# Step 14 of the attention alone with its own banks, first weight pieces two steps later, exponents on ScalarE beside the MLP

## The chip, the cores and the metric

The kernel runs on one core of one Trainium2 chip. The metric is the device time of one execution in microseconds (us); three runs of the kernel before gave a median of 999.9 us.

## The reference

Linear attention with random features over 4 batches, 8 heads, 576 positions and 64 dimensions, then two MLPs over the 2304 tokens of 512 values:

```python
def phi(x):
    proj = np.einsum('bhsd,md->bhsm', x, omega)          # m = 128
    h = proj - np.sum(x * x, axis=-1, keepdims=True) / 2.0
    return np.exp(h - np.max(h, axis=-1, keepdims=True)) / np.sqrt(m)
q_p, k_p = phi(q * scale), phi(k * scale)
kv, z = np.einsum('bhsm,bhsd->bhmd', k_p, v), np.sum(k_p, axis=2)
x = np.einsum('bhsm,bhmd->bhsd', q_p, kv) / (np.einsum('bhsm,bhm->bhs', q_p, z)[..., None] + 1e-06)
x = x.transpose(0, 2, 1, 3).reshape(2304, 512)
h = x @ w_in                                             # 512 x 2048
x = (np.maximum(h, 0.0) + alpha * np.minimum(h, 0.0)) @ w_out
out = ((x @ w_a) * (x @ w_b)) @ moe2_w_out               # 512 x 1536, back to 512
```

The weights reach the kernel as 64-bit floats, and every MLP product is made of three 32-bit matmuls: high by high, high by low and low by high part.

## The kernel before

The order of the program is the order of each engine: nothing is reordered behind the text. So what stands ahead in the code stands ahead in each engine's queue.

**Weights.** The 68 weight pieces (128x512 doubles, 512 KB) are fetched by SyncE into `raw` (three buffers) and decoded to a pair wh, wl by `Decoder.piece`. A double is two 32-bit words, L and H. `start` makes z from H by a multiplication with 2^-112 on GpSimd (POOL, L126). `piece` then goes on: VectorE (DVE) shifts z (L144), puts the sign in (a, L148), takes the exponent alone (c, L150) and scales L by it (c, L152); ScalarE (ACT) rounds a to wh (L154); POOL, or VectorE where the planner says so, makes a - wh (L155) and wl (L156). `D_.go(3)` takes up to three of a piece's four parts, `D_.go()` one more; `D_.step(x)` gives a step the credit of x pieces. z of the next piece is started as soon as the shift of the one before is issued.

**Attention.** It runs in steps of one tile of 128 positions for k and one for q (a q tile runs 6 steps or more behind the k tile). A step is: `attn_1`, projections into a pair of PSUM banks (pp, L543); `a_max`, the maxima of each part on VectorE (nm, L552); `loads`, the fetches that belong to the step; `a_exp`, exponentials on ScalarE (ph, L566); `attn_2`, parts of a weight piece, kv matmuls (L579), the quotient num/den (nd L613; rc, rc, xn on VectorE L617 to L620), the transposes of q's features (tp L594) and their copy phT (L597 on VectorE or L599 on ScalarE); `attn_3`, the transposes of the result (xp L632) and their copy into xT (L638 on VectorE, L640 on ScalarE).

**Banks.** Five shared banks (`psp`) hold pp, tp, nd, xp and later the MLP's h in turn. In the stage of the attention alone there are two more (`psx`), which the even steps take for their pp; when that stage ends they become the MLP's y.

**Stages.** Steps below `SPLIT_AT` = 14 run alone. Then the first MLP goes over chunks of 256 tokens (`A.run`), and `inside` puts one attention step into each of its f-steps: maxima and exponentials stand between the leaky step h (L285) and the parts gh, gl (L296, L293). Before that, the chunk of x is split into xh (ScalarE, L245) and xl (VectorE or POOL, L248). Behind 140 us mostly, a second program part runs the rest of the MLPs over chunks of 512 ("X phase").

**The planner.** `pick` chooses among engines by a running sum of estimated work: the way whose most loaded engine is least loaded. `passed` lets time go by. A change of an estimate so changes later choices.

Of the kernel before, what the change touches and what calls it, by code (L numbers as in the profile page):

```python
# [9 lines left out]
F32 = mybir.dt.float32  # L10
F32R = mybir.dt.float32r
U32 = mybir.dt.uint32
AF = mybir.ActivationFunctionType
ALU = mybir.AluOpType
# [4 lines left out]
P = 128  # L19
# [9 lines left out]
TT = 5  # L29
VC = 4 * (D + 1)  # L30
EPS = 1e-6
SPLIT_AT = 14
WARM = 7
Q_LAG = 6
CI = 256
# [6 lines left out]
NS = 28  # L42
NS1 = 20

DEC0 = (0.0, 0.3, 0.5)
DEC1 = 1.0
RATE_A = 0.55
RATE_A2 = 0.5
# [5 lines left out]
def tile_kernel(ctx: ExitStack, tc: tile.TileContext, qT, kT, v1, omT, wbits, alpha, out):  # L54
# [44 lines left out]
    class Decoder:  # L99


        def __init__(self):
            self.free = {}
            self.raw = {}
            self.ready = 0
            self.next = 0
            self.credit = 0.0
            self.gen = None
            self.z = {}
            self.ahead = True  # L110

        def load(self, p, after=False):
            if p < NP and p not in self.raw:
# [6 lines left out]
        def start(self, p):  # L120

            if p >= NP or p in self.z:
                return
            self.load(p)
            z = dec.tile([P, DM], U32, tag="z", name=f"z{p}")
            nc.gpsimd.tensor_scalar(out=z.bitcast(F32), in0=self.raw[p][:, :, 1].bitcast(F32), scalar1=2.0 ** -112,  # L126
                                    scalar2=None, op0=ALU.mult)
            load["pool"] += 0.8
            self.z[p] = z

        def piece(self, p):
# [86 lines left out]
    class Mlp:  # L218
# [20 lines left out]
        def split(self, ph, o, n, k):  # L239
            if (ph, o, k) in self.xs:  # L240
                return
            src = xT[:, k, o:o + n]
            hi = self.px.tile([P, self.cap], F32R, tag="xh", name=f"xh{ph}_{o}_{k}")[:, :n]
            lo = self.px.tile([P, self.cap], F32R, tag="xl", name=f"xl{ph}_{o}_{k}")[:, :n]
            nc.scalar.activation(hi, src, AF.Copy)  # L245
            load["act"] += n / 1000
            way = pick({"dve": 1.2 * n / 1000}, {"pool": 2.5 * n / 1000})
            (nc.vector, nc.gpsimd)[way].tensor_tensor(out=lo, in0=src, in1=hi.bitcast(F32), op=ALU.subtract)  # L248
            self.xs[ph, o, k] = (hi, lo)

# [416 lines left out]
    def loads(s):  # L667
        if s < 4:

            if s == 0:  # L670
                load_k(1)
            elif s == 1:
                D_.load(0, True)
                load_q(0)
            elif s == 2:
                load_v(1)
            elif s == 3:
                D_.load(1, True)
                load_q(1)
        elif s in ev["k"]:  # L680
            u, t = ev["k"][s]
            if t == 0 and u + 1 < U:
                load_k(u + 1)
            if t == 2 and u + 1 < U:
                load_v(u + 1)
        if s in ev["q"]:
            u, t = ev["q"][s]
            if t == 4 and u + 2 < U:
                load_q(u + 2)
# [32 lines left out]
    if True:  # L722
# [3 lines left out]
        for s in range(SPLIT_AT):  # L726
# [2 lines left out]
            pj = attn_1(s)  # L729
            nm = a_max(*pj)  # L730
            loads(s)
            a_exp(*pj, nm)
            if s == 3:
                D_.start(0)
            if s == Q_LAG + 1:
                nc.sync.dma_start(out=nalpha, in_=alpha)
            attn_2(s)
            attn_3(s)
            for k in range(KT):
                if s > x_step[k // 2, (CI - 1) // P]:  # L740
                    A.split(0, 0, CI, k)
        nc.vector.tensor_scalar(out=nalpha, in0=nalpha, scalar1=-1.0, scalar2=None, op0=ALU.mult)
    st_z.close()

    with st_m:
        A.banks((psp[0], "ps"))
        nxt_s = [SPLIT_AT]
        due = [0.0]

# [17 lines left out]
        def attn_more():  # L767
            attn_next()
            A.flush()
# [26 lines left out]
                due[0] -= 1  # L796
                attn_more()

        for k in range(KT):
            ready(CI, k)  # L800
            A.split(0, 0, CI, k)
        attn_more()
        A.run(work0, beside, ready)
        while nxt_s[0] < steps:
            attn_more()
# [79 lines left out]
```

## Time and profile before

| | |
|---|---|
| runs | 998.64, 999.9, 1001.19 us (median 999.9) |
| the profiled execution's own time | 998.33 us |
| its span | 996.5 us, 15871 instructions |
| PE busy | 975.1 us (98%) |
| VectorE, ScalarE, POOL busy | 497.7, 398.3, 354.1 us |
| moved by DMA | 75.16 MB, mean 75 GB/s |

The span is that of the profiled execution; its time is 1.8 us more. Busy is the time in which an engine worked; PE's sequence of matmuls is nearly closed, so an engine other than PE matters where PE waits for it. In the views below a row begins with its start in us and its length; what stands in square brackets is the idle time of the engine ahead of it and what ended it.

### The profile page before, as it was taken

To read this page: it belongs to the slowest core of one execution; us is meant where nothing else is said; L and a number is where in the kernel's file an instruction comes from. 1 tells how busy PE (TensorE), PEld (TensorE's weight loads), DVE (VectorE), ACT (ScalarE), POOL (GpSimd) and SP (SyncE) were. 2 spreads that over 40 slices of the span, in tenths; PEclk is the share of its full clock that TensorE was granted. 3 is DMA by queue.
4 is the path that set the end of the run, shared out by engine and by line. 5 is a ranking of instruction groups with operands and counts; after the bars stand their busy time and mean duration, and the time that the engine had idled before them with its cause. 6 is when DMAs were issued, how large, how long until landed. Compare 5 with 4: busy or idle time off the path is not lost.

```text
span 996.5 us, 15871 instructions
## 1 busy us (share of the span) xinstructions
PE 975.1 (98%) x6414; PEld 831.8 (83%) x6414; DVE 497.7 (50%) x943; ACT 398.3 (40%) x960; POOL 354.1 (36%) x257
## 2 busy tenths in 40 slices
PE   7889999999999999999999999999999999999998
PEld 6778889999888888898888888898888888898886
DVE  5878875554457665556446435344143523222132
ACT  6867777654444444444433322232132321121110
POOL 3687750000077655454153543443144430000100
PEclk9999999999999999999999999999999999999999
DMA  8544333000123151322121103022030302011021
GB/s 307 165 139 160 112 137 96 23 1 23 47 81 106 64 165 47 103 67 64 44 85 43 43 22 106 21 86 64 0 107 22 127 1 85 20 45 64 1 85 42
DMA packets 27449, 75.16 MB, mean 75 GB/s; under 512 B 2288, under 2 KB 5616, under 8 KB 27376
## 3 DMA queue, kind: packets, MB, share of 16 engines
q1 hardware_dynamic: 27232, 74.02, 22.3%
q8 instruction: 50, 0.82, 0.3%
q14 instruction: 23, 0.19, 0.1%
q10 hardware_dynamic: 144, 0.13, 0.0%
HBM read 59.99 MB, written 14.16 MB: 74 GB/s over the span
## 4 chain that ended last, share of the span: by engine, by line
PE 89%; ACT 5%; DVE 4%; issue 1%; POOL 1%; DMA 1%; SPq 0%; ACTq 0%; POOLq 0%; DVEq 0%
PE ab L259 30%; PE y L326 19%; PE h L259 18%; PE o L395 15%; ACT ph L566 2%; PE tp L594 1%; PE nd L613 1%; PE kv L579 1%; DVE a L148 1%; DMA v<-in_v 1%; PE xp L632 1%; DVE h L285 1%; ACT wh L154 1%; ACT phT L599 1%; POOL xl L248 0%
## 5 line engine op out<-in xcount | busy, mean ns | idle before, releaser
L155 POOL TENSOR_TENSOR a<-a,wh 128x512 f32<-128x512 f32 x68 | 105.7, 1555 | 285.4 <-ACT wh L154 282.8
L259 PE MATMUL ab<-xh,wh 128*128 128x512 f32 (+1 forms) x480 | 177.2, 369 | 0.0
L259 PE MATMUL ab<-xh,wl 128*128 128x512 f32 (+1 forms) x480 | 177.2, 369 | 0.0
L259 PE MATMUL ab<-xl,wh 128*128 128x512 f32 (+1 forms) x480 | 177.0, 369 | 0.0
L259 PE MATMUL h<-xh,wh 128*128 128x512 f32 (+1 forms) x384 | 132.4, 345 | 2.3 <-ACT ph L566 1.3
L259 PE MATMUL h<-xl,wh 128*128 128x512 f32 (+1 forms) x384 | 129.8, 338 | 2.2 <-POOL xl L248 1.8
L326 PE MATMUL y<-gh,wh 128*128 128x512 f32 (+1 forms) x384 | 131.0, 341 | 0.0
L326 PE MATMUL y<-gh,wl 128*128 128x512 f32 (+1 forms) x384 | 129.4, 337 | 0.0
L326 PE MATMUL y<-gl,wh 128*128 128x512 f32 (+1 forms) x384 | 129.4, 337 | 0.0
L259 PE MATMUL h<-xh,wl 128*128 128x512 f32 (+1 forms) x384 | 129.3, 337 | 0.0
L248 POOL TENSOR_TENSOR xl<-xT,xh 128x512 fp32r<-128x512 f32 (+1 forms) x37 | 39.6, 1077 | 234.1 <-ACT xh L245 234.1
L126 POOL TENSOR_SCALAR z<-raw 128x512 f32<-128x512 f32 x68 | 108.1, 1590 | 17.6 <-DMA raw<-in_w 17.6
L285 DVE SCALAR_TENSOR_TENSOR h<-u,nalpha,h 128x256 f32<-128x256 f32 (+1 forms) x96 | 59.6, 621 | 100.7 <-ACT h L284 99.7
L380 DVE TENSOR_TENSOR ab<-a,ab 128x512 f32<-128x512 f32 (+1 forms) x60 | 38.5, 641 | 141.2 <-PE ab L259 140.9
L259 PEld LDWEIGHTS ab<-xl,wh 128*128 128x128 f32 x480 | 90.4, 188 | 16.2
L259 PEld LDWEIGHTS ab<-xh,wh 128*128 128x128 f32 x480 | 90.4, 188 | 15.9
L259 PEld LDWEIGHTS ab<-xh,wl 128*128 128x128 f32 x480 | 90.4, 188 | 15.7
L156 POOL TENSOR_TENSOR wl<-a,c 128x512 fp32r<-128x512 f32 x68 | 90.7, 1334 | 5.3
L266 ACT ACTIVATE gh<-ab 128x512 fp32r<-128x512 f32 (+1 forms) x60 | 33.3, 555 | 135.9 <-DVE ab L380 135.9
L395 PE MATMUL o<-wh,gh 128*128 128x512 f32 x216 | 84.6, 392 | 0.0
L395 PE MATMUL o<-wh,gl 128*128 128x512 f32 x216 | 84.5, 391 | 0.0
L395 PE MATMUL o<-wl,gh 128*128 128x512 f32 x216 | 84.4, 391 | 0.0
(319 smaller groups left out, 1653.2 us busy)
## 6 DMA issues: line engine op xcount, KB each, us to landing
raw<-in_w SPq DMA_DIRECT2D x68, 512.0 KB, 3.7
v<-in_v SPq DMA_DIRECT2D x8, 650.0 KB, 5.9
q<-in_qT SPq DMA_DIRECT2D x8, 576.0 KB, 3.8
out<-opl SPq DMA_DIRECT2D x18, 256.0 KB, 2.0
yp<-ypart SPq DMA_DIRECT2D x4, 1024.0 KB, 6.6
opart<-op SPq DMA_DIRECT2D x4, 1024.0 KB, 5.0
opl<-opart SPq DMA_DIRECT2D x4, 1024.0 KB, 5.7
k<-in_kT SPq DMA_DIRECT2D x7, 576.0 KB, 4.4
```

The lines of the kernel that those rows point to most:

```text
L126: nc.gpsimd.tensor_scalar(out=z.bitcast(F32), in0=self.raw[p][:, :, 1].bitcast(F32), scalar1=2.0 ** -112, scalar2=None, op0=ALU.mult)
L148: stt(out=a, in0=H, scalar=0x80000000, in1=z, op0=ALU.bitwise_and, op1=ALU.bitwise_or)
L155: eng.tensor_tensor(out=a, in0=a, in1=hi.bitcast(F32), op=ALU.subtract)
L156: eng.tensor_tensor(out=lo, in0=a, in1=c, op=ALU.add)
L248: (nc.vector, nc.gpsimd)[way].tensor_tensor(out=lo, in0=src, in1=hi.bitcast(F32), op=ALU.subtract)
L259: nc.tensor.matmul(hp, lhsT=w_[:, ks], rhs=r_, start=(i == 0), stop=(i == 3 * KT - 1))
L266: nc.scalar.activation(gh, g, AF.Copy)
L285: nc.vector.scalar_tensor_tensor(out=hp, in0=u_, scalar=nalpha[:, f:f + 1], in1=hp, op0=ALU.mult, op1=ALU.add)
L326: nc.tensor.matmul(ys[e], lhsT=w_[:, es], rhs=r_, start=(first and i == 0 and head), stop=(last and i == 2 and tail))
L380: nc.vector.tensor_tensor(out=pp[1], in0=a_, in1=pp[1], op=ALU.mult)
L395: nc.tensor.matmul(os_[t], lhsT=w_[:, ts_], rhs=r_, start=(i6 == 0 and i == 0), stop=(i6 == 5 and i == 2))
L566: nc.scalar.activation(ph[:, 2 * pr + j], pair[j][:, o + pr], AF.Exp, bias=nm[:, j, o + pr:o + pr + 1])
```

## The change

Six edits. `SPLIT_AT` goes from 14 to 15: step 14 is one of the alone stage, with the psx banks. `DEC0`, the credit of pieces that a step of the alone stage gets (up to step 2, up to step 5, from step 6), goes from 0, 0.3, 0.5 to 0, 0, 0.6: pieces 0 to 4 are then decoded in steps 7, 9, 11, 12 and 14, where it was 6, 8, 10, 12 and 14. The first two pieces are fetched at steps 4 and 5 (behind q0, v1, q1 in SyncE's queue), no longer at 1 and 3, and the first z is started at step 5. The splits of x move from the end of a step to between its maxima and its exponentials. xl of a 256-token chunk is always made on VectorE. From step 15 on, z is made on ScalarE (a copy with scale 2^-112), and the planner counts 0.65 on ScalarE for it, or 1.6 on POOL where it was 0.8. The block that stood ahead of `A.run` and ran one attention step there is gone.

```diff
@@ -29,7 +29,7 @@
 TT = 5
 VC = 4 * (D + 1)
 EPS = 1e-6
-SPLIT_AT = 14
+SPLIT_AT = 15
 WARM = 7
 Q_LAG = 6
 CI = 256
@@ -42,7 +42,7 @@
 NS = 28
 NS1 = 20
 
-DEC0 = (0.0, 0.3, 0.5)
+DEC0 = (0.0, 0.0, 0.6)
 DEC1 = 1.0
 RATE_A = 0.55
 RATE_A2 = 0.5
@@ -108,6 +108,7 @@
             self.gen = None
             self.z = {}
             self.ahead = True
+            self.scalar = False
 
         def load(self, p, after=False):
             if p < NP and p not in self.raw:
@@ -123,9 +124,13 @@
                 return
             self.load(p)
             z = dec.tile([P, DM], U32, tag="z", name=f"z{p}")
-            nc.gpsimd.tensor_scalar(out=z.bitcast(F32), in0=self.raw[p][:, :, 1].bitcast(F32), scalar1=2.0 ** -112,
-                                    scalar2=None, op0=ALU.mult)
-            load["pool"] += 0.8
+            H = self.raw[p][:, :, 1].bitcast(F32)
+            if self.scalar:
+                nc.scalar.activation(z.bitcast(F32), H, AF.Copy, scale=2.0 ** -112)
+                load["act"] += 0.65
+            else:
+                nc.gpsimd.tensor_scalar(out=z.bitcast(F32), in0=H, scalar1=2.0 ** -112, scalar2=None, op0=ALU.mult)
+                load["pool"] += 1.6
             self.z[p] = z
 
         def piece(self, p):
@@ -244,7 +249,8 @@
             lo = self.px.tile([P, self.cap], F32R, tag="xl", name=f"xl{ph}_{o}_{k}")[:, :n]
             nc.scalar.activation(hi, src, AF.Copy)
             load["act"] += n / 1000
-            way = pick({"dve": 1.2 * n / 1000}, {"pool": 2.5 * n / 1000})
+
+            way = pick({"dve": 1.2 * n / 1000}, *([] if self.pair else [{"pool": 2.5 * n / 1000}]))
             (nc.vector, nc.gpsimd)[way].tensor_tensor(out=lo, in0=src, in1=hi.bitcast(F32), op=ALU.subtract)
             self.xs[ph, o, k] = (hi, lo)
 
@@ -670,12 +676,10 @@
             if s == 0:
                 load_k(1)
             elif s == 1:
-                D_.load(0, True)
                 load_q(0)
             elif s == 2:
                 load_v(1)
             elif s == 3:
-                D_.load(1, True)
                 load_q(1)
         elif s in ev["k"]:
             u, t = ev["k"][s]
@@ -683,6 +687,8 @@
                 load_k(u + 1)
             if t == 2 and u + 1 < U:
                 load_v(u + 1)
+            if s in (4, 5):
+                D_.load(s - 4, True)
         if s in ev["q"]:
             u, t = ev["q"][s]
             if t == 4 and u + 2 < U:
@@ -729,21 +735,23 @@
             pj = attn_1(s)
             nm = a_max(*pj)
             loads(s)
+
+            for k in range(KT):
+                if s > x_step[k // 2, (CI - 1) // P]:
+                    A.split(0, 0, CI, k)
             a_exp(*pj, nm)
-            if s == 3:
+            if s == 5:
                 D_.start(0)
             if s == Q_LAG + 1:
                 nc.sync.dma_start(out=nalpha, in_=alpha)
             attn_2(s)
             attn_3(s)
-            for k in range(KT):
-                if s > x_step[k // 2, (CI - 1) // P]:
-                    A.split(0, 0, CI, k)
         nc.vector.tensor_scalar(out=nalpha, in0=nalpha, scalar1=-1.0, scalar2=None, op0=ALU.mult)
     st_z.close()
 
     with st_m:
         A.banks((psp[0], "ps"))
+        D_.scalar = True
         nxt_s = [SPLIT_AT]
         due = [0.0]
 
@@ -796,10 +804,6 @@
                 due[0] -= 1
                 attn_more()
 
-        for k in range(KT):
-            ready(CI, k)
-            A.split(0, 0, CI, k)
-        attn_more()
         A.run(work0, beside, ready)
         while nxt_s[0] < steps:
             attn_more()
```

On VectorE at steps 6 to 8 (nm are the maxima, the three numbers being q or k slot, unit and tile of the step; z, a, c are piece 0's decode). Before:

```order
L552 TENSOR_REDUCE nm(0, 1, 1)_328<-pp(1, 1)_False_318 128x4
L552 TENSOR_REDUCE nm(0, 1, 1)_328<-pp(1, 1)_False_319 128x4
L144 TENSOR_SCALAR z_265<-z_265 128x512
L148 SCALAR_TENSOR_TENSOR a_343<-raw_200,z_265 128x512
L150 TENSOR_SCALAR c_344<-a_343 128x512
L152 SCALAR_TENSOR_TENSOR c_344<-raw_200,c_344 128x512
L552 TENSOR_REDUCE nm(0, 1, 2)_373<-pp(1, 2)_False_363 128x4
L552 TENSOR_REDUCE nm(0, 1, 2)_373<-pp(1, 2)_False_364 128x4
```

Now:

```order
L558 TENSOR_REDUCE nm(0, 1, 1)_328<-pp(1, 1)_False_318 128x4
L558 TENSOR_REDUCE nm(0, 1, 1)_328<-pp(1, 1)_False_319 128x4
L558 TENSOR_REDUCE nm(0, 1, 2)_360<-pp(1, 2)_False_350 128x4
L558 TENSOR_REDUCE nm(0, 1, 2)_360<-pp(1, 2)_False_351 128x4
L149 TENSOR_SCALAR z_307<-z_307 128x512
L153 SCALAR_TENSOR_TENSOR a_378<-raw_274,z_307 128x512
L155 TENSOR_SCALAR c_379<-a_378 128x512
L157 SCALAR_TENSOR_TENSOR c_379<-raw_274,c_379 128x512
```

The decode of the first piece has moved behind the maxima of the next step.

In SyncE's queue at the start (the transfers in the order in which they are issued). Before:

```order
L510 DMA k_183<-in_kT 128x1152
L117 DMA raw_200<-in_w 128x1024
L524 DMA q_203<-in_qT 128x1152
L517 DMA v_229<-in_v 128x1300
L117 DMA raw_254<-in_w 128x1024
L524 DMA q_257<-in_qT 128x1152
L510 DMA k_302<-in_kT 128x1152
L117 DMA raw_341<-in_w 128x1024
```

Now:

```order
L516 DMA k_183<-in_kT 128x1152
L530 DMA q_200<-in_qT 128x1152
L523 DMA v_226<-in_v 128x1300
L530 DMA q_251<-in_qT 128x1152
L118 DMA raw_274<-in_w 128x1024
L516 DMA k_297<-in_kT 128x1152
L118 DMA raw_299<-in_w 128x1024
L523 DMA v_363<-in_v 128x1300
```

The first two raw stand behind both q and v1.

On VectorE in step 14 (xT is the copy of an earlier result, xl the low halves of x's k tiles 2 and 3, nm the maxima of step 14). Before:

```order
L638 COPY xT<-xp_1_756 128x2x128
L742 TENSOR_SCALAR nalpha<-nalpha 128x16
L248 TENSOR_TENSOR xl_0_2_766<-xT,xh_0_2_765 128x256
L248 TENSOR_TENSOR xl_0_3_770<-xT,xh_0_3_769 128x256
L552 TENSOR_REDUCE nm(0, 2, 4)_781<-pp(2, 4)_False_773 128x1
L552 TENSOR_REDUCE nm(0, 2, 4)_781<-pp(2, 4)_False_773 128x2
L552 TENSOR_REDUCE nm(0, 2, 4)_781<-pp(2, 4)_False_774 128x1
L552 TENSOR_REDUCE nm(0, 2, 4)_781<-pp(2, 4)_False_774 128x2
L144 TENSOR_SCALAR z_655<-z_655 128x512
```

Now:

```order
L644 COPY xT<-xp_1_756 128x2x128
L558 TENSOR_REDUCE nm(0, 2, 4)_768<-pp(2, 4)_False_760 128x1
L558 TENSOR_REDUCE nm(0, 2, 4)_768<-pp(2, 4)_False_760 128x2
L558 TENSOR_REDUCE nm(0, 2, 4)_768<-pp(2, 4)_False_761 128x1
L558 TENSOR_REDUCE nm(0, 2, 4)_768<-pp(2, 4)_False_761 128x2
L254 TENSOR_TENSOR xl_0_2_774<-xT,xh_0_2_773 128x256
L254 TENSOR_TENSOR xl_0_3_778<-xT,xh_0_3_777 128x256
L149 TENSOR_SCALAR z_663<-z_663 128x512
```

The maxima have moved ahead of the two low halves; nalpha's sign change comes later.

On ScalarE in step 15 (ph the exponentials, wh and phT what PE and POOL wait for, u the first reading of the MLP's h). Before:

```order
L566 ACTIVATE ph_0_874<-pp(3, 0)_False_857,nm(0, 3, 0)_866 128x128 x2
L566 ACTIVATE ph_4_875<-pp(3, 0)_False_857,nm(0, 3, 0)_866 128x128
L566 ACTIVATE ph_0_874<-pp(3, 0)_False_858,nm(0, 3, 0)_866 128x128 x2
L566 ACTIVATE ph_4_875<-pp(3, 0)_False_858,nm(0, 3, 0)_866 128x128
L585 ACTIVATE kvp_134<-kv_593 128x260
L154 ACTIVATE wh_82<-a_884 128x512
L599 ACTIVATE phT_2_919<-tp_2_914 128x512
L640 ACTIVATE xT<-xp_3_921 128x2x128
L245 ACTIVATE xh_256_0_925<-xT 128x256
L283 ACTIVATE u_0_1_942<-h_0_1_929 128x256
```

Now:

```order
L572 ACTIVATE ph_0_874<-pp(3, 0)_False_857,nm(0, 3, 0)_866 128x128 x2
L572 ACTIVATE ph_4_875<-pp(3, 0)_False_857,nm(0, 3, 0)_866 128x128
L572 ACTIVATE ph_0_874<-pp(3, 0)_False_858,nm(0, 3, 0)_866 128x128 x2
L572 ACTIVATE ph_4_875<-pp(3, 0)_False_858,nm(0, 3, 0)_866 128x128
L129 ACTIVATE z_887<-raw_789 128x512
L591 ACTIVATE kvp_134<-kv_590 128x260
L159 ACTIVATE wh_82<-a_884 128x512
L605 ACTIVATE phT_2_919<-tp_2_914 128x512
L646 ACTIVATE xT<-xp_3_921 128x2x128
L250 ACTIVATE xh_256_0_925<-xT 128x256
L289 ACTIVATE u_0_1_942<-h_0_1_929 128x256
```

One 128x512 activation, z of the next piece, has come in between the exponentials and kvp. (The new rows have the line numbers of the changed file.)

## Rows read from the trace of the kernel before

**Rows 1.** Busy time of each engine in three stretches; columns: stretch, length, engines, clock, DMA.

```profile
14.72:46.34 31.62, 24.51 (x406) 20.85 (x408) 28.17 (x64) 26.07 (x88) 19.25 (x15) 1.00 0.66 233
46.34:140.00 93.66, 87.92 (x1088) 79.29 (x1090) 78.85 (x182) 68.11 (x214) 70.60 (x51) 1.00 0.44 151
140.00:996.50 856.50, 850.53 (x4773) 721.17 (x4770) 385.95 (x679) 296.56 (x639) 262.03 (x186) 1.00 0.18 58
```

**Rows 2.** VectorE's waits, 14.72 to 46.34 us: total, times, longest us.

```profile
DVE xl L248 <- ACT xh L245: 1.5, 2, 1.2
DVE nm(0, 1, 1)_328 L552 <- ACT ph L566: 0.9, 1, 0.9
DVE nm(0, 2, 0)_508 L552 <- PE pp(2, 0)_False L543: 0.9, 1, 0.9
```

**Rows 3.** Timeline around the first two pieces: start, length, operation.

```profile
11.64 1.53 POOL L126 TENSOR_SCALAR z<-raw 128x512 f32<-128x512 f32 x1 [10.35 <-DMA raw<-in_w]
...
16.24 0.69 PE L579 MATMUL kv<-v,ph 128*64 128x65 f32 x16 [1.61 <-DMA v<-in_v]
...
17.30 1.60 POOL L126 TENSOR_SCALAR z<-raw 128x512 f32<-128x512 f32 x1 [4.13 <-DMA raw<-in_w]
17.41 0.61 PE L543 MATMUL pp(1, 2)_False<-om,q 64*128 64x128 f32 x8
...
18.50 1.27 DVE L552 TENSOR_REDUCE nm(0, 1, 2)_373<-pp(1, 2)_False 128x4 f32<-128x512 f32 x2
...
21.03 0.74 DVE L144 TENSOR_SCALAR z<-z 128x512 uint32<-128x512 uint32 x1
...
28.23 0.42 DVE L144 TENSOR_SCALAR z<-z 128x512 uint32<-128x512 uint32 x1
```

**Rows 4.** DMA issues on the page: count, KB each, us to landing.

```profile
raw<-in_w SPq DMA_DIRECT2D x68, 512.0 KB, 3.7
v<-in_v SPq DMA_DIRECT2D x8, 650.0 KB, 5.9
q<-in_qT SPq DMA_DIRECT2D x8, 576.0 KB, 3.8
```

**Rows 5.** PE's waits, 14 to 47 us.

```profile
PE pp(2, 4)_False L543 <- ACT ph L566: 1.2, 1, 1.2
```

**Rows 6.** PE's waits, 47 to 140 us.

```profile
PE h L259 <- POOL xl L248: 1.7, 1, 1.7
```

**Rows 7.** VectorE, 140 to 300 us, by line and form: busy us, mean ns.

```profile
L597 DVE COPY phT<-tp 128x512 f32<-128x512 f32 x3 | 2.0, 680 | 0.0
```

**Rows 8.** Timeline of VectorE before 71 us.

```profile
69.92 0.49 DVE L285 SCALAR_TENSOR_TENSOR h<-u,nalpha,h 128x256 f32<-128x256 f32 x1 [0.82 <-ACT h L284]
70.86 0.42 DVE L293 TENSOR_TENSOR gl<-h,gh 128x256 fp32r<-128x256 f32 x1 [0.45 <-ACT gh L296]
```

**Rows 9.** The chain of waits, 46 to 140 us: start, us, what.

```profile
50.84 0.49 ACT phT L599
...
84.83 1.16 PE pp(4, 1)_False L543 x14
...
90.74 0.87 PE pp(4, 2)_False L543 x12
...
128.18 0.27 ACT phT L599
```

**Rows 10.** Timeline of ScalarE, one round.

```profile
79.51 0.39 ACT L283 ACTIVATE u<-h 128x256 f32<-128x256 f32 x1
...
83.65 0.65 ACT L154 ACTIVATE wh<-a 128x512 fp32r<-128x512 f32 x1
84.18 0.59 ACT L599 ACTIVATE phT<-tp 128x512 f32<-128x512 f32 x1
...
84.92 0.40 ACT L283 ACTIVATE u<-h 128x256 f32<-128x256 f32 x1
```

**Rows 11.** ScalarE by line, 46 to 140 us: busy, mean ns, idle before.

```profile
L154 ACT ACTIVATE wh<-a 128x512 fp32r<-128x512 f32 x15 | 9.6, 640 | 2.7 <-DVE a L148 2.5
```

## The prediction

> **What bounds the kernel now.** I read first the busy time of the engines in three stretches [rows 1]: the attention alone up to the first MLP matmuls, the MLP with attention between (to 140 us), and the rest. The reader is to see what PE leaves free in each, since PE sets the end: 31.62 - 24.51 = 7.1 us in the first, 93.66 - 87.92 = 5.7 us in the second, 856.50 - 850.53 = 6.0 us in 856 us of the third. PE works nearly all the time from 46 us on, and no step taken from another engine helps there unless PE waits for it. In the first stretch VectorE is busy 28.17 of 31.62 us and ScalarE 26.07: VectorE bounds it. Second, VectorE's waits in that stretch [rows 2]: 1.5 us for the high halves of x (xh), 0.9 for the exponentials of step 6, 0.9 for projections of step 10; 3.3 in all, which with 28.17 busy fills the stretch. Third, the timeline of the first pieces [rows 3] with the sizes of the transfers [rows 4]. Fourth, PE's waits: at the maxima's banks of step 14 [rows 5] and for one low half of x [rows 6]. Last, the chain of waits beside the MLP [rows 9], which says where ScalarE holds PE. All clocks read 1.00 in these stretches [rows 1], so durations need no correction.
>
> The profiled run took 998.33 us, the median of the three runs is 999.9. I sum against 998.33 and add the 1.57 us between them at the end.
>
> **Entry, steps 6 to 14.** VectorE's work here changes by counting: one low half (xl) more and one copy of xT less, which cancel within 0.02 us by their equal shapes (128x256), and two copies phT of 128x512 that the planner now gives to VectorE. Such a copy took 680 ns on VectorE later in the run [rows 7]: 2 x 0.68 = +1.36. The splits of k tiles 2 and 3 now stand behind the maxima of step 14, not ahead of them, so ScalarE makes xh while VectorE does maxima, and the 1.5 us wait [rows 2] goes: -1.5. The other two waits, for exponentials and projections, I leave as they are.
>
> The wait that is added is for the first piece. In the rows before, POOL's z starts when its raw has landed: 11.64 for piece 0 and 17.30 for piece 1, and both waited for the DMA. Between the two landed q0, v1 and raw1: 576 + 650 + 512 = 1738 KB in 5.66 us, 307 KB a us [rows 3, 4]. In the new order raw0 stands behind k1, q0, v1, q1. Without raw0 ahead, q0's transfer starts 512/307 = 1.67 us earlier, at 9.97; then q0, v1, q1 and raw0, 2314 KB, take 7.54 and land at 17.5. POOL's z takes 1.53 [rows 3], so it is there at 19.0. VectorE: v1 lands at 9.97 + 1226/307 = 13.96, so PE's wait of 1.61 for v goes, and the projections pp(1,2), which ended at 17.41 + 0.61, end at 16.4; the maxima of step 7 take 1.27 [rows 3], and VectorE comes to z at 17.7. It waits about 1.2 to 1.3; I take 1.2. Behind that waiting shift stand, on VectorE, all decode operations of piece 0 and the maxima of step 8; PE's projections of the next step wait for these only through exponentials. On POOL the same wait costs nothing, for it has 12 us idle in the stretch [rows 1].
>
> Sum of the entry: 1.36 - 1.5 + 1.2 = **+1.1**. At best z is in time and the other two waits go as well: 1.36 - 3.3 = -1.9. At worst the xh wait stays in another place: +2.6.
>
> The own banks of step 14 take away PE's wait of 1.2 at pp(2, 4) [rows 5]. I give it nothing: PE runs ahead there, while the first MLP matmul still wants the exponentials' ScalarE turn and VectorE's low halves, which end when VectorE ends. Cover: VectorE's chain; if VectorE were faster, at most this 1.2 would show, and it lies inside the lower bound above.
>
> **Low halves beside the MLP.** One xl on POOL held PE for 1.7 us [rows 6], the largest single wait behind 46 us. On VectorE it takes 0.42 (as the gl of the same shape) and can stand at 69.1, where VectorE sits idle 0.82 us ahead of h at 69.92 [rows 8]. Next late is gl, which ends at 70.86 + 0.42 = 71.28 [rows 8] for the matmuls after it: some 0.4 of the wait stays. **-1.3**; bounds -1.7 (nothing late) and -0.4 (xl and gl queue up behind each other on VectorE, twice 0.42 more than this).
>
> **Exponents on ScalarE.** From step 15 on every piece adds one 128x512 activation to ScalarE, between the exponentials and kvp, wh, phT. Its issue interval is that from wh to phT, 83.65 to 84.18: 0.53; I take 0.52 [rows 10]. It doesn't hurt at its own place (POOL and VectorE want z only a step later) but pushes wh and phT back. The chain of waits shows where this reaches PE: it runs over a phT on ScalarE at five places behind 47 us, the first at 50.84, the last at 128.18 [rows 9]; at the first three PE's projections, as pp(4, 1) at 84.83, wait for the bank that phT empties, at the other two ScalarE itself goes on from phT to the readings of h. Five times 0.52 is 2.6. Against it stands that ScalarE's wh waited for VectorE's a, 2.7 us over 15 pieces, 0.18 each [rows 11], time in which z would be free: 5 x (0.52 - 0.18) = 1.7. I take the middle, **+2.1**, bounds 1.7 and 2.6 for these places, 0 if PE had more slack than the chain says, and the rival below if other places join. Off the path: 62 such activations move in all, of them 47 behind 140 us, where PE is idle 6.0 of 856 us [rows 1]; nothing for them, covered by PE. POOL, which loses 66 operations, gains nothing by itself: its wl ends late only where wh was late.
>
> **Sum:** 1.1 - 1.3 + 2.1 = +1.9. Profiled 1000.2; median 1000.2 + 1.57 = **1001.8**.
>
> **Rivals.** *A, slower: ScalarE's round becomes the bound.* Between two u of neighbouring steps ScalarE needs 79.51 to 84.92, 5.41 us [rows 10]. With z 5.93. PE's round from pp(4, 1) to pp(4, 2) is 84.83 to 90.74, 5.91 [rows 9]. They are level; from the point at which z takes more than 0.5 in most steps, or PE's round is shorter than this one, each of the 15 pieces costs its 0.52: 7.8 - 2.7 hidden [rows 11] = 5.1. Sum 1.1 - 1.3 + 5.1 = +4.9: 1004.8. For it: the level rounds and three engines in one chain. Against it: in many steps PE's wait list names no phT at all, and PE idles only 5.7 us in this stretch [rows 1].
>
> *B, faster: the entry opens up.* Own banks and earlier k and q let projections run ahead, VectorE never waits, and z is hidden in ScalarE's gaps: -1.9 - 1.3 + 0 = -3.2: 996.7. For it: three waits in the entry are real and in VectorE's way [rows 2]. Against it: the piece arrives later by my sum, and VectorE's added copies are sure.
>
> *C, relief for VectorE.* L144, the first decode step, took 0.74 at 21.03 beside POOL's work, and 0.42 at 28.23 [rows 3]. With POOL's z gone, the decode up to wh could be 0.32 shorter at each of the five places: 2.1 - 1.6 = 0.5, sum +0.3, median 1000.2. Against it: POOL's a and wl remain, and they are two of three POOL operations of a piece. The Trainium skill, "SBUF — State Buffer", § "Who interferes with whom", says that VectorE in a two-port mode or with two SBUF inputs and GpSimd lock each other out of a shared port, while ScalarE has its own; by that rule z on ScalarE gives VectorE time back, and the 0.74 beside 0.42 agrees with it in kind, though no run here separates it from chance.
>
> *That the change doesn't do what it says:* step 14's wait for a bank could come back one step later, since step 15 takes the shared banks that step 13 and the transposes just used. That is in my entry (nothing counted for the 1.2), and so no case of its own.
>
> **Chances.** What a measurement of this kernel can tell from no change is about 0.3%, 3.0 us. My forecast 0.41, C 0.15, A 0.30, B 0.14. Forecast and C lie within 3 us of 999.9, A above, B just below. So faster 0.14, same 0.56, slower 0.30. The range goes from 997.5 (most of B's way) to 1005.0 (A); about 0.1 stays out on each side.
>
> **What would show it.** In the profile of the changed kernel: POOL's first z starts near 17.5, and VectorE's first shift waits about 1 us for it; the xh wait is gone from VectorE's list; the stage's last decode ends near 47.4, where it was 46.3; PE's wait for POOL's xl is gone, with 0.4 for gl in its place; PE's waits at pp for ScalarE's phT are larger by some 0.5 at each of a handful of places; L144 beside the MLP is nearer to 0.42. Wrong would be: a first z before 15 us (the queue's order doesn't set landing), the entry shorter by over 1 us (B), or a wait for ScalarE in nearly every step between 47 and 140 us (A).

## The result, and the profile after

The changed kernel took 1006.4 us, the median of 6 runs (1004.77 to 1008.28), beside 1000.0 for the kernel before: ratio 1.0062, 95% interval 1.0049 to 1.0074. The forecast was 1001.8, with a range up to 1005.0 and a chance of 0.30 for slower by over 0.3%. It went to the side of rival A, but mostly not by A's mechanism.

| | before | changed |
|---|---|---|
| median | 1000.0 | 1006.4 us |
| profiled execution, its span | 998.33, 996.5 | 1006.19, 1004.4 us |
| PE busy | 975.1 | 980.1 us |
| ScalarE, POOL busy | 398.3, 354.1 | 430.0, 256.9 us |
| mean granted clock | 1.00 | 0.994 |

PE's matmuls stand in the same order in both, so the lag of a matmul is the difference of its starts. It is 3.3 us at the first MLP matmul (h: 44.59 before, 47.93 now), 4.4 at the transposes of step 15 (xp), 7.1 at 141 us and 7.8 at the end. The rows of h and xp, before:

```profile
44.59 0.38 PE L259 MATMUL h<-xh,wh 128*128 128x256 f32 x1 [1.29 <-ACT ph L566]
...
48.93 0.44 PE L632 MATMUL xp<-ident,xn 128*128 128x128 f32 x2 [0.34 <-ACT ph L566]
```

Now:

```profile
47.93 0.36 PE L265 MATMUL h<-xh,wh 128*128 128x256 f32 x1
...
53.30 0.44 PE L638 MATMUL xp<-ident,xn 128*128 128x128 f32 x2 [1.03 <-ACT ph L572]
```

PE's wait for exponentials has moved: it stood ahead of h (1.29) and stands now, longer than it was there, ahead of xp (1.03 for 0.34). The lag at h alone so leaves out 1.0 of what the entry costs.

The same three stretches of the changed kernel as in [rows 1] (stretch, length, then busy time of PE, PE's loads, VectorE, ScalarE, POOL; the granted clock, DMA):

```profile
14.72:46.34 31.62, 25.45 (x390) 21.39 (x388) 26.78 (x59) 23.34 (x79) 20.34 (x14) 0.90 0.68 229
46.34:140.00 93.66, 85.76 (x1053) 76.91 (x1049) 76.86 (x182) 72.59 (x221) 36.99 (x29) 1.00 0.43 144
140.00:1004.40 864.40, 856.93 (x4851) 727.19 (x4849) 381.68 (x697) 327.69 (x700) 198.84 (x143) 1.00 0.18 59
```

The clock of the first stretch is 0.90, where it was 1.00. Beside the MLP PE is idle 7.9 us (5.7 before), behind 140 us 7.5 (6.0 before). In stretches of 2 us the clock shows three places at half speed, 1.2 in place of 2.4 GHz (same columns):

```profile
10.00:12.00 2.00, 2.00 (x26) 1.66 (x24) 0.70 (x4) 1.01 (x5) 0.00 (x0) 0.50 0.90 266
...
28.00:30.00 2.00, 2.00 (x19) 1.77 (x18) 1.86 (x5) 1.06 (x3) 1.56 (x2) 0.50 0.03 12
44.00:46.00 2.00, 2.00 (x16) 1.44 (x17) 1.54 (x5) 2.00 (x9) 2.00 (x2) 0.50 0.58 229
```

VectorE's longest waits in the entry, which answer to [rows 2]:

```profile
DVE z L149 <- POOL z L132: 1.3, 1, 1.3
DVE nm(0, 1, 1)_328 L558 <- ACT ph L572: 0.9, 1, 0.9
DVE nm(0, 1, 2)_360 L558 <- ACT ph L572: 0.9, 1, 0.9
```

The wait for xh is gone and the one for z is there, as forecast. The timeline of the entry (answers to [rows 3] and [rows 5]):

```profile
19.40 1.54 POOL L132 TENSOR_SCALAR z<-raw 128x512 f32<-128x512 f32 x1 [18.11 <-DMA raw<-in_w]
...
20.97 0.43 DVE L149 TENSOR_SCALAR z<-z 128x512 uint32<-128x512 uint32 x1 [1.35 <-POOL z L132]
...
24.75 0.34 PE L585 MATMUL kv<-v,ph 128*64 128x65 f32 x4 [2.12 <-ACT ph L572]
...
38.01 1.26 POOL L161 TENSOR_TENSOR wl<-a,c 128x512 fp32r<-128x512 f32 x1
...
38.23 2.11 DVE L254 TENSOR_TENSOR xl<-xT,xh 128x256 fp32r<-128x256 f32 x2
...
42.61 0.69 PE L619 MATMUL nd<-kvp,phT 128*64 128x65 f32 x16 [2.29 <-ACT phT L605]
```

Three things are to be seen. The first z starts at 19.40, not at 17.5. Two low halves of x, 0.43 each when alone, take 2.11 us beside POOL's wl. And PE stands for 2.12 and 2.29 us, in front of the second and third half-clock stretches.

PE's waits from 48 to 145 us that concern the prediction (answers to [rows 6] and [rows 9]):

```profile
PE pp(4, 1)_False L549 <- ACT phT L605: 0.8, 1, 0.8
PE h L265 <- DVE xl L254: 0.7, 1, 0.7
...
PE pp(5, 4)_False L549 <- ACT phT L605: 0.5, 1, 0.5
PE pp(4, 4)_False L549 <- ACT phT L605: 0.5, 1, 0.5
...
PE pp(3, 2)_False L549 <- ACT phT L605: 0.5, 1, 0.5
```

The wait for POOL's xl is gone there; those for phT have grown. One new wait stands in the late part, where the prediction counted nothing (PE's waits, 145 us to the end; before, the same line had 0.2):

```profile
PE h L265 <- POOL xl L254: 1.2, 1, 1.2
```

### The profile page after: what moved, and what is told of

Its sections match the earlier page's. It is cut to its first block, busy times and chain, and to the rows that moved or that the text cites. A ratio compares the mean times of both kernels' runs of the same rounds, so it can differ in the third digit from the quotient of the medians.

```text
span 1004.4 us, 15863 instructions
## 1 busy us (share of the span) xinstructions
PE 980.1 (98%) x6414; PEld 836.1 (83%) x6414; DVE 489.6 (49%) x953; ACT 430.0 (43%) x1016; POOL 256.9 (26%) x191
## 4 chain that ended last, share of the span: by engine, by line
PE 89%; ACT 5%; DVE 4%; issue 1%; DMA 1%; POOL 1%; ACTq 0%; DVEq 0%; POOLq 0%
PE ab L265 30%; PE y L332 19%; PE h L265 18%; PE o L401 15%; ACT ph L572 2%; PE tp L600 1%; PE kv L585 1%; PE nd L619 1%; DVE xl L254 1%; PE xp L638 1%; DVE h L291 1%; DMA raw<-in_w 1%; ACT wh L159 0%; ACT z L129 0%; ACT phT L605 0%
## 5 line engine op out<-in xcount | busy, mean ns | idle before, releaser
L160 POOL TENSOR_TENSOR a<-a,wh 128x512 f32<-128x512 f32 x68 | 103.4, 1521 | 472.1 <-ACT wh L159 437.5
L265 PEld LDWEIGHTS h<-xl,wh 128*128 128x128 f32 x384 | 72.7, 189 | 11.1 <-POOL xl L254 1.6
L254 POOL TENSOR_TENSOR xl<-xT,xh 128x512 fp32r<-128x512 f32 (+1 forms) x33 | 42.3, 1287 | 151.5 <-ACT xh L250 151.5
```

The costliest lines, as they stand in the source:

```text
L160: eng.tensor_tensor(out=a, in0=a, in1=hi.bitcast(F32), op=ALU.subtract)
L265: nc.tensor.matmul(hp, lhsT=w_[:, ks], rhs=r_, start=(i == 0), stop=(i == 3 * KT - 1))
```

## The experiments

All times are medians; where a run has an interval, it is of its ratio to the kernel before in the same session (999.6 to 1000.3 us). Between two changed versions no interval was worked out; most have four to nine runs that spread over 1 to 4 us, so a difference of 1.5 us or less between them is not clear of noise. The theories: A, ScalarE's round with z holds PE at a handful of places, and VectorE's chain sets the entry; B, the z is hidden and all comes from the shifted entry; C, the half clock is the loss; L, low halves on VectorE stand still beside POOL.

**z on POOL again (e1).** The planner's estimates and every other instruction stay.

```diff
-                nc.scalar.activation(z.bitcast(F32), H, AF.Copy, scale=2.0 ** -112)
+                nc.gpsimd.tensor_scalar(out=z.bitcast(F32), in0=H, scalar1=2.0 ** -112, scalar2=None, op0=ALU.mult)
```

> The changed kernel, but with z made on POOL again from step 15 on (the planner's estimates as in the change, so that every other instruction keeps its engine and place). Theory A (ScalarE's round decides in several steps): in the changed trace PE lags the one before by 0.5 to 0.8 us more at each of five projections that wait for phT (62, 90, 111, 135, 141 us), 3.1 in all, and 1.0 more at one wait for exponentials at 53.3. All of this should go: some 3 to 4 us, 1002.4 to 1003.4, and the lag at 145 us falls from 7.1 to about 3.5. Theory B (z is hidden; the waits for phT come from the later and differently shifted entry): the time stays within 1 us of 1006.4 and the waits stay.

1003.0 us (1.0013 to 1.0034): 3.4 less than the change. In its trace the lag falls at the projections (at 62 us in the changed kernel) instead of growing, and is 2.2 at 76 us and still 2.6 at 264. A, not B.

**The kernel before with z on ScalarE alone (e6).** The estimates stay as before.

```diff
+            if self.scalar:
+                nc.scalar.activation(z.bitcast(F32), H, AF.Copy, scale=2.0 ** -112)
+            else:
+                nc.gpsimd.tensor_scalar(...)
...
+        D_.scalar = True
         A.run(work0, beside, ready)
```

> The kernel before with z on ScalarE from the MLP's first f-step on and nothing else (planner's estimates and all other places as before). Theory A (z on ScalarE holds PE at five projections, 0.5 to 0.8 us each): +3 to +3.5, 1003.0 to 1003.5, independent of the entry. Rival (half of it is made up by the POOL that comes free): +1 to +2. The kernel with z on ScalarE, xl on VectorE and the old entry took 1005.5, so if this one takes 1003, moving xl costs 2 by itself.

1002.8 us (1.0013 to 1.0031), 2.5 more than before, a little below A. Its profiled clock is 1.00 throughout, as in the profiled execution of before, so the two traces compare matmul by matmul. The lag grows at seven projections, 2.9 in all: at 84.8, 104.6, 128.5 and 134.0 us (times of before) by 0.55, 0.56, 0.57 and 0.51, at 51.4, 57.2 and 79.5 by 0.19, 0.30 and 0.25. At 71.7 us 0.3 comes back. PE's waits of this kernel, 47 to 140 us:

```profile
PE pp(4, 1)_False L547 <- ACT phT L603: 0.8, 1, 0.8
...
PE pp(4, 4)_False L547 <- ACT phT L603: 0.5, 1, 0.5
...
PE pp(3, 2)_False L547 <- ACT phT L603: 0.5, 1, 0.5
PE pp(5, 4)_False L547 <- ACT phT L603: 0.5, 1, 0.5
```

**The old entry under the change (e2)**: steps, fetches, credits and splits as before; z on ScalarE with its estimates and xl on VectorE as in the change.

```diff
-SPLIT_AT = 15
-DEC0 = (0.0, 0.0, 0.6)
+SPLIT_AT = 14
+DEC0 = (0.0, 0.3, 0.5)
...
             elif s == 1:
+                D_.load(0, True)
                 load_q(0)
...
+        for k in range(KT):
+            ready(CI, k)
+            A.split(0, 0, CI, k)
+        attn_more()
         A.run(work0, beside, ready)
```

> The changed kernel with the old entry: step 14 beside the MLP on shared banks, raw pieces fetched at steps 1 and 3, the old credits, splits at the end of a step; z stays on ScalarE beside the MLP and xl on VectorE. Theory A: the entry is worth its lag at the first MLP matmul, 3.3 us, so 1003.1, PE's clock reads 1.00 in all of the entry, and the waits for phT beside the MLP stay (some 3 us). Theory B (entry shifts cause the phT waits too): the whole of the loss goes, 999 to 1000.

1005.5 us (1.0036 to 1.0062): 0.9 less than the change, a miss for both theories. The old entry with xl on VectorE is itself no good one (e7, below), and its clock read 0.50 too, from 24 to 27 and 45 to 47 us. The lag at the projections was there as in the change. Against that kernel (e7, 1001.2) z with its estimates costs 4.3.

**The old fetches and credits only (e3).**

```diff
-DEC0 = (0.0, 0.0, 0.6)
+DEC0 = (0.0, 0.3, 0.5)
...
+                D_.load(0, True)
                 load_q(0)
...
-            if s in (4, 5):
-                D_.load(s - 4, True)
...
-            if s == 5:
+            if s == 3:
                 D_.start(0)
```

> The changed kernel with the first two pieces fetched at steps 1 and 3 again and decoded by the old credits; own banks, splits and z on ScalarE as in the change. Theory A (the entry is VectorE's chain: 1.35 us wait for z of piece 0, 1.36 us by which two low halves on VectorE took 2.11 instead of 0.75 us beside POOL's wl and z, the rest the half clock): the z wait goes, the low halves stay in conflict or move: 1 to 2 us better, 1004.4 to 1005.4. Theory C (the late pieces cause the long PE waits, these the half clock, and the clock the loss): the clock reads 1.00 and the full 3.3 go: about 1003.

1003.1 us (1.0021 to 1.0041): 3.3 less. The price agrees with C's number. C's reason is not shown by it: the profiled execution, at 1005.65 us the slowest of the nine, ran at half clock from 7 to 17 us. The low halves of step 12 took 0.76, not 2.11.

**Old fetches, new credits (e10).** As e3, with `DEC0 = (0.0, 0.0, 0.6)` left.

> The changed kernel with the first two pieces fetched at steps 1 and 3 and z started at step 3, as before, but decoded by the new credits (steps 7, 9, 11, 12, 14). It splits the 3.3 us that late pieces cost: if the wait for z (1.35 us) is what costs, it goes here and the time falls by 1.3 to 3.3 us, to 1003 to 1005. If the new places of the decode cost (POOL's wl and z lie beside the two low halves of step 12, 2.11 in place of 0.76 us), the pair still takes 2.1 here and the time stays within 1.5 of 1006.4.

1003.4 us (1.0025 to 1.0052), runs within 0.8 of each other: 3.0 less than the change, so the late fetch is what costs. The new credits, with the two copies phT on VectorE that come with them (0.68 each here, none in e3), cost 0.3 against e3, which is within the noise. The two low halves took 2.21 here and PE still waited 2.3 at nd, so that place costs little by itself. z was early (timeline):

```profile
13.13 1.54 POOL L132 TENSOR_SCALAR z<-raw 128x512 f32<-128x512 f32 x1 [11.85 <-DMA raw<-in_w]
...
19.27 0.42 DVE L149 TENSOR_SCALAR z<-z 128x512 uint32<-128x512 uint32 x1
```

VectorE comes to z at 19.27 without waiting, 1.7 us ahead of the change; at the first MLP matmul (45.13 against 47.93) it is 2.8. From 6 to 40 us its clock was 1.00; the change had two half-clock stretches there.

**Idle matmuls in three waits of the changed kernel (e4)**, so that PE does not stand still.

```diff
+        if s in (1, 9):
+            fill_pe(s, 6)
         if s in ev["kv"]:
             a_kv(*ev["kv"][s])
+        if s == 13:
+            fill_pe(s, 8)
```

> The changed kernel with idle matmuls (128x128 on a tile of zeros, their bank overwritten by the next quotient) put into three of PE's waits of the entry, 6 before kv in steps 1 and 9 and 8 before nd in step 13, so that PE does not stand still for 1.7 to 2.3 us there. Theory A (VectorE bounds the entry): the granted clock stays nearer to 1.00 in the entry, yet the time falls by less than 1 us, 1005.4 to 1006.4. Theory C (half clock is the loss of the entry): 2.5 to 3.5 us better, 1003 to 1004.

1005.2 us (1.0040 to 1.0065): 1.2 less, between the theories and not clear of noise. The test did not do in step 13 what it was meant to. The idle matmuls of steps 1 and 9 ran inside PE's waits, but those of step 13 (nd<-warm) waited for phT themselves, started only at 41.01 and held the quotient's own matmuls back to 43.50:

```profile
41.01 2.56 PE L613 MATMUL nd<-warm 128*128 128x128 f32 x16 [2.33 <-ACT phT L605]
...
43.50 1.14 PE L628 MATMUL nd<-kvp,phT 128*64 128x65 f32 x16
```

What it does show stands ahead of that. In its profiled execution (1007.1 us, the slowest of the five) the first two half-clock stretches are gone, and the maxima of step 13 start 1.6 us earlier than in the change. In e10, also at full clock up to there, they start another 1.2 earlier. The row in the change, in e4 and in e10:

```profile
43.26 1.28 DVE L558 TENSOR_REDUCE nm(0, 2, 3)_714<-pp(2, 3)_False 128x4 f32<-128x512 f32 x2
...
41.65 1.28 DVE L558 TENSOR_REDUCE nm(0, 2, 3)_727<-pp(2, 3)_False 128x4 f32<-128x512 f32 x2
...
40.48 1.28 DVE L558 TENSOR_REDUCE nm(0, 2, 3)_714<-pp(2, 3)_False 128x4 f32<-128x512 f32 x2
```

So in these executions the two half-clock stretches cost 1.6 of the 2.8 us by which e10 is ahead, and the late fetch at full clock 1.2. The idle matmuls of step 13 then took the gain of e4 back: h starts at 48.31. This is one execution of each kernel.

**The kernel before in another execution (b1).**

> The kernel before, unchanged, profiled in another execution. Theory P (the profiled execution of before was a lucky one: its clock read 1.00 all through the entry and its 998.33 us lies 1.7 below the median; other executions have stretches at half clock in the entry as well): the clock reads below 1.00 somewhere before 47 us and the first MLP matmul starts 1 to 2.5 us later than 44.59. Theory Q (the half clock belongs to the change): 1.00 throughout and 44.6 again.

999.9 us, the median of before, at a mean clock of 0.997. Two rows of its 2 us stretches:

```profile
10.00:12.00 2.00, 2.00 (x26) 1.66 (x26) 0.54 (x4) 0.98 (x4) 0.00 (x0) 0.51 1.01 386
22.00:24.00 2.00, 1.88 (x16) 1.43 (x16) 1.93 (x4) 2.00 (x10) 2.00 (x2) 0.55 0.65 234
```

Its lag behind the profiled execution of before is 1.5 us from 24.6 us to the end, at h too (46.12). So P is right: the half clock belongs to both kernels and comes in some executions only; the execution on which the prediction rests had none. The 1.57 us that the prediction added at the end is about this.

**The kernel before with xl on VectorE alone (e7).**

```diff
-            way = pick({"dve": 1.2 * n / 1000}, {"pool": 2.5 * n / 1000})
+            way = pick({"dve": 1.2 * n / 1000}, *([] if self.pair else [{"pool": 2.5 * n / 1000}]))
```

> The kernel before with the low halves of the 256-token chunks always on VectorE and nothing else. Theory by the prediction: the wait of 1.7 us at 71.7 goes, 0.4 stays: -1.3, 998.7. Theory now (the trace of the changed kernel gives 1.4 of the 1.8 gained back at once, in matmuls of h and y behind it, and two low halves on VectorE in the entry took 2.11 instead of 0.75 us): 0 to +1.5, 1000 to 1001.5.

1001.2 us (1.0004 to 1.0024): slower by 0.9, where the prediction's term said 1.3 faster. The lag falls by 1.9 at 71.74 and grows by 1.0 in the next matmuls. In the entry the first two low halves took 2.08 beside wl:

```profile
40.05 2.08 DVE L248 TENSOR_TENSOR xl<-xT,xh 128x256 fp32r<-128x256 f32 x2
...
40.52 1.33 POOL L156 TENSOR_TENSOR wl<-a,c 128x512 fp32r<-128x512 f32 x1
```

**Own banks, splits between and xl on VectorE (e8)**: the change without late pieces and without z on ScalarE; fetches, credits and POOL's estimate of z are as before.

```diff
+            elif s == 1:
+                D_.load(0, True)
...
-        D_.scalar = True
```

> The change without its late pieces and without z on ScalarE: what stays is step 14 in the alone stage with its own banks, the splits between maxima and exponentials, and xl on VectorE. If the prices measured so far add up (late pieces 3.3, z 3.4, from 1006.4): 999.7, the same as before. Rival (they overlap, since each price was taken with the other there): 1001 to 1002.

998.8 us (0.9973 to 0.9992): 1.5 better than before, and better than both expectations. In this step order the low halves do not meet wl and took 0.76 for two.

**The same with POOL allowed for xl (e11).**

```diff
-            way = pick({"dve": 1.2 * n / 1000}, *([] if self.pair else [{"pool": 2.5 * n / 1000}]))
+            way = pick({"dve": 1.2 * n / 1000}, {"pool": 2.5 * n / 1000})
```

> Own banks for step 14 and the splits between maxima and exponentials, nothing else: pieces, z and the choice for low halves as before. The version with xl on VectorE took 998.8. Theory L with the lag of its trace (the low halves on VectorE give back 0.9 us at 72 us and cost nothing in this entry, where they took 0.76 for two): 999.5 to 1000. Rival (VectorE better off without them): 998.

1001.4 us (1.0001 to 1.0019). That is above both expectations: xl on VectorE is worth 2.6 with own banks, and banks and splits without it cost 1.3. Between the two traces 1.1 of the 2.6 shows; e8's profiled execution was the slowest of its eleven.

**The change with POOL allowed for xl (e5)**, by the same edit.

> The changed kernel with POOL allowed again for the low halves of the 256-token chunks (the planner then puts the first pair, step 12, and most others on POOL). Theory L (a low half on VectorE reads two tiles of SBUF and stands still while POOL's wl runs: 1.33 us where one took 0.43, 1.4 to 1.5 us for the pair in step 12): the entry becomes 1 to 2 us shorter, the wait of 1.7 us for POOL's xl at 72 us comes back, net gain 0 to 1.5, 1005 to 1006.4. Rival (VectorE's lock costs nothing, the pair is hidden): only the wait comes back, 1007.2 or more.

1007.8 us (1.0066 to 1.0094): 1.4 more, on the rival's side of the two. With four runs, which overlap those of the change, it is not clear of noise that xl on VectorE gains in the change; the 1.4 would be about what the prediction gave it.

**The low halves of step 12 moved behind that step's decode (e12).**

```diff
-                    A.split(0, 0, CI, k)
+                    A.split(0, 0, CI, k, late if s == 12 else None)
...
         D_.go(3)
+        while late:
+            late.pop(0)()
```

> The changed kernel with the two low halves of step 12 moved on VectorE behind the four decode operations of that step; POOL's wl, beside which they took 2.11 us, is then over. Theory L (the low half stands still while POOL runs an operation on two tiles, and this holds up the decode, wh, phT and PE's nd for 2.3 us): the pair takes 0.75 to 0.9, PE's wait at nd falls from 2.3 to about 1, and the time by 1 to 1.5 us to about 1005. Rival (the pair meets another POOL operation at its new place, or the wait at nd has another cause): 1006 to 1006.5.

1007.9 us (1.0066 to 1.0092): 1.5 more than the change as medians, with overlapping runs; no gain in any case, against the expectation. At their new place the two met POOL's a - wh and wl one after the other, and the shift that now stood at their old place met wl (timeline):

```profile
38.34 1.27 POOL L161 TENSOR_TENSOR wl<-a,c 128x512 fp32r<-128x512 f32 x1
38.55 1.34 DVE L149 TENSOR_SCALAR z<-z 128x512 uint32<-128x512 uint32 x1
...
41.72 1.71 POOL L160 TENSOR_TENSOR a<-a,wh 128x512 f32<-128x512 f32 x1 [0.43 <-ACT wh L159]
...
42.21 2.90 DVE L254 TENSOR_TENSOR xl<-xT,xh 128x256 fp32r<-128x256 f32 x2
43.51 1.32 POOL L161 TENSOR_TENSOR wl<-a,c 128x512 fp32r<-128x512 f32 x1
```

The edit missed its aim, but it shows how the length hangs on POOL: 0.76, 2.11 and 2.90 us for the same two operations, beside none, one and two of POOL's operations on two tiles. It does not show what the 2.11 costs the kernel. The rival's first half was right.

**Own banks with idle matmuls (e9)**: e8 and, ahead of kv, eight in step 1 and four in step 8.

```diff
+FILL = {1: 8, 8: 4}
...
+        if s in FILL:
+            fill_pe(s, FILL[s])
         if s in ev["kv"]:
             a_kv(*ev["kv"][s])
```

> The version with own banks, splits between and xl on VectorE (998.8), with idle matmuls ahead of kv in steps 1 (eight) and 8 (four), where PE stood still for 2.05 and 0.9 us in its trace and after which the clock read 0.50 from 8.2 to 12.5 and 22 to 29 us. Theory C (the half clock costs the entry about 1.5 to 2 us, in this kernel and in the one before, whose undisturbed execution has h at 44.6 and another one at 46.1): 997 to 997.5 with the clock at 1.00. Theory A (VectorE bounds the entry whatever the clock): 998.3 to 999.

997.6 us (0.9967 to 0.9985), 11 runs within 0.65 us where e8 spread over 3.6. The clock of its entry (stretches as above):

```profile
10.00:12.00 2.00, 1.95 (x33) 1.47 (x31) 1.02 (x7) 1.81 (x8) 0.03 (x1) 1.00 0.96 377
12.00:46.00 34.00, 29.87 (x472) 25.23 (x474) 28.96 (x69) 28.25 (x96) 20.58 (x15) 1.00 0.68 240
```

By its median this version is the fastest of all, 2.4 us better than before, near C. The three executions of e8 whose mean clock read 1.000 took 997.0 to 997.7 us, so the idle matmuls gain nothing beyond a full clock in every execution.

**The kernel before with the same idle matmuls (b3)**, by the same edit.

> The kernel before with idle matmuls (128x128 on a tile of zeros) ahead of kv in steps 1 (eight) and 8 (four) and nothing else. Theory C (stretches at half clock, which some executions of before have in the entry and some do not, make part of its spread): 998.3 to 999, the clock at 1.00, the runs within 1.5 us of one another where they spread over 3.5 without. Rival (the gain of the filled version came from its own banks alone): 1000.1 and the same spread.

999.9 us (0.9994 to 1.0012): no gain; the runs lie within 1.5 us, those of before in that session within 3.8. C is right on the spread and wrong on the median. In its profile the entry ran at full clock and a half-clock stretch came at 74 us instead.

## Why the prediction was wrong, point by point

**What failed** is the price of two terms. The late fetch was priced at VectorE's wait alone, and z on ScalarE with a discount and without the choices that its estimates move. The runs form a chain in which each version is the one ahead of it with one step more: 1000.0 before, 1001.4 (e11), 998.8 (e8), 1003.1 (e3), 1003.4 (e10), 1006.4 the change. The forecast for the same steps:

| step | forecast | measured |
|---|---|---|
| banks and splits (e11), xl on VectorE (e8): -1.5 for the xh wait, -1.3 for xl | -2.8 | -1.2 |
| z on ScalarE with the planner's estimates (e3) | +2.1 | +4.3 |
| new credits, with two copies phT on VectorE (e10) | +1.4 | +0.3 |
| late fetch (the change) | +1.2 | +3.0 |

The measured column adds up to 6.4 because it is a chain, which proves nothing of the order: xl is -2.6 here, -1.4 in the change and +0.9 alone. The first and third rows miss by 1.6 and 1.1 in opposite directions, which is luck.

**What bounds the kernel** held in part: ScalarE's round at a handful of places beside the MLP, PE elsewhere. In the entry it is not VectorE's chain alone. In e4 VectorE has the same work in the same order, and without the first two half-clock stretches it is at step 13 1.6 us earlier.

**The entry**: +1.1 forecast. The lag is 3.3 at h and 4.4 at xp of step 15, and 1.5 of it is the execution in which the kernel before was profiled (b1); like for like it is some 2.9, outside the bound of 2.6. By steps:

- *The late fetch* was mis-sized. The sum took VectorE's wait for the whole price. That wait was forecast at 1.2 and was 1.35, and at full clock the fetch costs 1.2 in the chain (e4 and e10). But undone, the fetch gives back 3.0 (change to e10), and in the traces the other 1.6 are the two half-clock stretches, where the prediction said that durations need no correction. The second, from 26 to 30 us, stands behind the 2.12 us that PE waits at kv for late exponentials, 0.7 at most in e10. That the late fetch also causes the first, from 8 to 13 us, is not shown; b1 has one there without it.
- *When raw0 lands* was wrong in its reason: I let it follow the transfers ahead of it at 307 KB a us, 17.5. The fetch waits for a small write by VectorE behind step 4's maxima, so it was issued at 13.78 and z started at 19.40. VectorE came to z at 19.6, not 17.7, so that both were 1.9 late and the wait came out near 1.2: in part luck.
- *The xh wait* went, as forecast (-1.5), and the same two low halves then took 2.11 in place of 0.76 beside wl. I counted operations and cancelled the added xl against a copy; what stands on POOL at that moment I did not look up. The rule that I cited for rival C works here against the change. By the Trainium skill, "SBUF — State Buffer", § "Who interferes with whom", a VectorE operation with two SBUF inputs and a GpSimd operation that reads SBUF contend. The trace agrees: 0.43 alone against 1.33 beside wl for one low half. That these 1.35 us reach the end is not shown: in e10, with 2.21, the step that brings them costs 0.3.
- *The two phT copies* took 0.67 and 0.68, the length that was forecast, but they came with the new credits, and all of these cost 0.3.
- *PE's wait at pp(2, 4)* went without a gain, as forecast, but something like the last rival came: PE waits for exponentials one step later. The lag grows by 1.0 to 1.4 between h and xp of step 15 in the change and in e1, e3, e8 and e10, and does not in e2, e6 and e7, which have the old entry.
- *The half clock* was in no term. The profiled execution of before had 1.00 everywhere, and I took that for the kernel's own state; b1 shows otherwise.

**Low halves beside the MLP**, -1.3 (bounds -1.7 to -0.4): the change gains 1.4 by it (e5), within the bounds but not clear of noise; with own banks the gain is 2.6 (e11 to e8). In the trace the lag falls by 1.8 at 74.80 and grows again by 1.5 in the next matmuls, where PE waits 0.7 for a pair that took 1.85 beside wl, and 0.3 for gh. The same edit alone costs 0.9 (e7): its price depends on what it meets on POOL.

**z on ScalarE**, +2.1 (bounds 1.7 to 2.6): 2.5 as median alone (e6), 3.4 in the change (to e1), 4.3 with the planner's estimates (e7 to e2, e8 to e3). The mechanism was right, place by place: all five places of [rows 9] showed, and 79.5 and 134.0 besides. The discount failed. I took off 0.18 a place because wh waited for VectorE's a [rows 11]; z took 0.57 of ScalarE's turn, and at four places the lag grew by 0.51 to 0.57 (e6), nearly all of it. Rival C's relief is in the same rows, though not from the row that I gave for it: the 0.74 of [rows 3] stood beside wl (20.22 to 21.49), which stays on POOL. VectorE and ScalarE, 46 to 140 us before and 46 to 145 us in the changed kernel, busy us and means in ns:

```profile
L144 DVE TENSOR_SCALAR z<-z 128x512 uint32<-128x512 uint32 x15 | 8.4, 558 | 0.0
```

Now:

```profile
L159 ACT ACTIVATE wh<-a 128x512 fp32r<-128x512 f32 x15 | 10.1, 672 | 0.1
...
L149 DVE TENSOR_SCALAR z<-z 128x512 uint32<-128x512 uint32 x16 | 6.6, 415 | 0.0
```

The shift is at 415 ns, down from 558 (439 where z alone moved, e6), so VectorE did get time back, and wh waits 0.1 for it, no longer 2.7. But ScalarE then has no gap left in which z could hide, and the relief shows nowhere in the time. Rival A, a full cost at each of 15 pieces, did not come.

**Behind 140 us**: nothing forecast, 0.8 measured (the lag goes from 7.1 to 7.8; it grows by 1.15 at 466 us and 0.47 of it comes back). The planner's other estimates for z gave seven more low halves of 128x512 in the late part to POOL (27, where it had 20); one held PE for 1.2 us. That wait is there in every version that keeps the estimates of the change, e1 too, and not in e6, e7, e8. No run changes the estimates alone, so the 0.8 is read from the trace. I priced the z that move and not the choices that the estimate moves.

## What to carry to other kernels

Look up what the neighbouring engine does at the very moment at which an operation is put, above all where both read two tiles: counting operations by engine missed a factor of three. A wait in front of a queue can cost more than itself: here PE stood still behind it, and a half-clock stretch followed. An estimate in a planner is an edit like any other. Idle matmuls that are to fill a wait must not wait for the same thing. And a trace at full clock is one execution: where PE has waits in its first 50 us, a second profile tells whether the first was typical.

## What the runs showed of the hardware

One low half of 128x256 on VectorE, 0.43 us, took 1.33 beside POOL's wl, which had begun 0.22 us ahead of it, and ended 0.28 us behind it; one that began 0.19 us ahead of wl kept its 0.43 (kernel before, 38.21). A pair took up to 2.90. The granted clock fell to 0.50 in the entry of both kernels, behind waits of PE (1.71, 2.12 and 2.29 us in the changed kernel; 1.85, and then twice 0.69, in b1), and in other executions of the same program not at all: the profiled one of before kept 1.00 behind waits of 1.45 and 1.61; with idle matmuls in such waits 11 runs agreed within 0.65 us.
